# One set of tiles over all 768 tokens, in-products of the groups in two halves of 384 columns, and a written load order for attention

## The chip, the core and the metric

The kernel runs on one core of a Trainium2 chip. The metric is device time in microseconds (us) of one execution; a run is repeated and the median is taken. TensorE does the matmuls (its instruction stream is PE in the profile, its weight loads PEld), VectorE (DVE), ScalarE (ACT) and GpSimd (POOL) do the elementwise work, SyncE (SP) issues the DMAs that bring data from HBM into SBUF. Results of matmuls land in PSUM, from where DVE and ACT take them.

## What is computed

A decayed linear attention over 2 batches, 8 heads, 768 tokens of head size 64, whose output is laid out as 1536 tokens of 512 features; then a gated MLP with 1536 hidden features and an MLP with 2048 hidden features and an ELU between its two matrices:

```
intra = einsum(qb, kb) * Dmask;  intra = einsum(intra, vb)          # per block of 64 tokens
inter = einsum(qb * lam_pow, kv_state)
kv_state = lam_block * kv_state + einsum(kb * rev_pow, vb)
x = attention output, (1536, 512)
x = (sigmoid(x @ w_gate) * (x @ w_val)) @ w_out                     # hidden 1536
h = x @ w_in;  x = where(h > 0, h, exp(min(h, 0)) - 1) @ w_out2     # hidden 2048
```

## The kernel before

All of it is recorded first and ordered afterwards. The code calls operations on a `Work` object, in the order in which they are written; `hazards` works out which operation must follow which, `run` plays the list with a table of costs, `issue` tries some settings and keeps the order with the earliest end. Each engine then gets its instructions in that order, and the real program waits on semaphores. So the order on every engine, SP's DMAs too, is the planner's, not that of the code. Since every operation is issued by one line, the profile's line column says L182 (the line in `call`) almost everywhere, and tiles, not lines, tell the work apart.

The tokens of both batches stand side by side: a tile has 2 batches times 768 tokens, cut in token ranges `s = 0` (256 tokens) and `s = 1` (512 tokens) with a tile each (`NS = (256, 512)`). The attention goes in six chunks `c` of 128 tokens. `scores(c)` makes the masked scores `pr` and the state update (PSUM tiles `st`), then the output of the chunk is summed in PSUM (`x`) from `pr` and the values (`x<-pr,nat`) and from the state `sn` and the decayed queries `ql` (`x<-ql,sn`). Between the two a small ACT operation on the tile `low` stands as a fence. `split_chunk` turns the chunk into a high and a low part (`x11h`, `x11l`, `x143h`, `xPh` and so on), the operands of the MLPs. `kd` are the keys with their decay, made by ACT from `nat`, the loaded keys and values; `tin` holds the loaded transposed keys and queries.

The two MLPs go in groups of 256 hidden features, 6 and 8 of them. A weight is fetched as raw 64-bit words into the one tile `w64` (`w_88`, `w_83` below), made into 32 bits by one ACT and two DVE operations (tile `w`), summed and split into high and low parts `h` and `l` of several tags by POOL, ACT and DVE. An **in-product** (`product`) computes one hidden group for one range of tokens by a scheme of seven products M1 to M7. Each of the seven is six matmuls of 128 by 128 weights (two row blocks `k`, and high times high, high times low, low times high), so 42 matmuls, each as many columns wide as the range has tokens. Their results stand in PSUM banks `A0/B0/C0` or `A1/B1/C1`; the profile's names for them are `warm`, `B` and `st`. DVE and ACT add them up with `wt` and write `sig`, which is split into `gh` and `gl`. An **out-product** (`unit`) multiplies `gh` and `gl` with the output weights `woh`, `wol`, always 512 columns wide (2 batches of 256 tokens), into PSUM tile `xu`; DVE adds it to `acc`.

Groups 1 to 4 of the gated MLP (products G and V) and groups 1 to 6 of the second MLP (product H) use `FULL`, one range of 256 and one of 512 columns; group 0, the last group of the first MLP and the first of the second use three ranges of 256; the last of all uses 512 and 256.

In the attention, chunk 2 is loaded into places of its own (`xPh1` and `sig1`), the others by turns into `gh1` and `gl1` and the two halves of `acc1`. SP waits before a DMA until the old contents of its target have been read.

Of the kernel before, what the change touches and what calls it, by code (L numbers as in the profile page):

```python
# [26 lines left out]
NS = (256, 512)  # L27
# [9 lines left out]
WORDS = 4096  # L37
# [90 lines left out]
class Work:  # L128
    MATMUL = {512: (229, 391), 384: (173, 335), 256: (120, 283)}
# [77 lines left out]
    def hazards(self):  # L207
        write, read, banks, tables = {}, {}, {}, {1: [], 2: []}
        holder, users, freed = {}, {}, {}
        for k, op in enumerate(list(self.ops)):  # L210
# [49 lines left out]
            if op.fence:  # L260
                before.add(self.ops.index(op.fence))
            before -= {-1, k}
            op.preds = sorted(before)

    def run(self, preds, key, backward=False, gate=None, stick=0, thrift=20000):
# [33 lines left out]
        for _ in range(sum(op.eng is not None for op in ops)):  # L299
# [45 lines left out]
            while done:  # L345
                x = done.pop()
                for s in after[x]:
                    f = ops[s].eng
                    ready = free[e] if f == e == "tensor" and x == k else end[x] + self.HANDOFF.get(f, 0)
# [49 lines left out]
def tile_decay_attention_two_mlps(  # L399
# [78 lines left out]
    def new_xops(s):  # L478
        n = NS[s]
        o = {}  # L480
        for t in ("11", "22"):
            for q in "hl":
                o[t, q] = sb.tile([P, 2, n], F32R, f"x{t}{q}{s}")
        for q in "hl":
            o["143", q] = sb.tile([P, 3, 2, n], F32R, f"x143{q}{s}")
            for k, t in enumerate("143"):
                o[t, q] = o["143", q][:, k]
            o["P", q] = sb.tile([P, KC, n], F32R, f"xP{q}{s}")
        return o
# [3 lines left out]
    def x_operand(ops, s, m):  # L493
        o = ops[s]
# [35 lines left out]
    FULL = ((0, 0, 256), (1, 0, 512))  # L530
    PARTS = ((0, 0, 256), (1, 0, 256), (1, 256, 256))

    def product(kind, w, ops, sig, r, which, gsplit=None, two=False):
        s, t0, n = r
        bank, wt = {}, None
        for m in ("M5", "M2") + ORDER[2:] if two else ORDER:
# [9 lines left out]
            bh, bl = (v[:, :, t0:t0 + n] for v in x_operand(ops, s, m))  # L546
# [5 lines left out]
            if wt is None:  # L552
                wt = sb.tile([P, NS[which]], F32, f"wt{which}", bufs=2)[:, :n]
# [5 lines left out]
            else:  # L559
                fh, b = {"M4": (1, 0), "M3": (0, 1), "M7": (0, 0), "M6": (1, 1)}[m]  # L560
                dst = sig[s][:, fh, b, t0:t0 + n]
# [10 lines left out]
                if gsplit is not None and m in ("M7", "M6"):  # L572
                    gsplit(s, fh, t0, n)

    def new_sig():
        return [sb.tile([P, 2, 2, NS[s]], F32, f"sig{s}") for s in range(2)]

# [4 lines left out]
    low = sb.tile([P, 2 * KC * NS[0]], F32, "acc0", name="low")  # L582
    nat = sb.tile([P, 2, 2, 2, H, D], F32, "acc1", name="nat")
# [8 lines left out]
    tin, nat_of = {}, {c: nat[:, int(c in (1, 4))] for c in (0, 1, 3, 4, 5)}  # L592

    def load(c):
        if c == 2:
            tin[c] = sb.tile([P, 2, 2, 2, 2, CH], F32, "xPh1", name="tin2")
            nat_of[c] = sb.tile([P, 2, 2, H, D], F32, "sig1", name="nat2")
        else:
            tin[c] = sb.tile([P, 2, 2, 2, 2, CH], F32, ("gh1", "gl1")[int(c in (1, 4))], name="tin")
        for to, src in ((tin[c].rearrange("p g b q i n -> p (g b q i n)"), att[c, 0]),  # L600
                        (nat_of[c].rearrange("p q b h e -> p (q b h e)"), att[c, 1])):
            for cols in (slice(0, 1024), slice(1024, 2048)) if c < 3 else (slice(0, 2048),):
                nc.sync.dma_start(out=to[:, cols], in_=src[:, cols])

    load(0)
    load(1)
    w64G = load_w(w_gate, 0)
    load(2)
# [36 lines left out]
    xops = [new_xops(0), new_xops(1)]  # L645
    prs, kds, sns = {}, {}, {}
    wG = wV = None
    sig = None
# [8 lines left out]
    def scores(c):  # L657
        prs[c] = []
        if c:
            sns[c] = sb.tile([P, 2, NP, D], F32, f"wt1_{c % 2}", name="sn")  # L660
# [37 lines left out]
    for c in range(NCH):  # L698
        more = c + 1 < NCH
        s, t0 = (0, c * CH) if c < 2 else (1, (c - 2) * CH)  # L700
        scores(c)
        if c in (1, 2, 4):
            load({1: 3, 2: 4, 4: 5}[c])
        if more:
            kd = kds[c] = sb.tile([P, 2, H, D], F32, ("gh0", "gl0")[c % 2], name="kd")
# [40 lines left out]
        split_chunk(xops[s], slice(t0, t0 + CH), xs, xa)  # L746
        if c == 0:
            wG = prep_pair(w_gate, 0, nc.gpsimd, nc.vector, nc.gpsimd, raw=w64G)
        if c == 1:
            wV = prep_pair(w_val, 0, nc.gpsimd, nc.vector, nc.gpsimd)  # L750
            sig = new_sig()
        if c in (1, 3, 5):
            r = PARTS[c // 2]
# [5 lines left out]
    acc = [sb.tile([P, 2, KC, NS[s]], F32, f"acc{s}") for s in range(2)]  # L759

    def new_g(big=None):
        g = []
        for s in range(2):
            if s and big:
                g.append([[sb.tile([P, 2, NS[s]], F32R, f"x{t}{q}{s}", name=f"g{q}{s}") for t in big] for q in "hl"])
            else:
                tl = [sb.tile([P, 2, 2, NS[s]], F32R, f"g{q}{s}") for q in "hl"]
                g.append([[v[:, fh] for fh in range(2)] for v in tl])
        return g

    def splitter(sig, g, eng=None, eng0=None):
        def f(s, fh, t0=0, n=None):
            ts = slice(t0, t0 + (n or NS[s]))
            h, l, x = (v[:, :, ts] for v in (g[s][0][fh], g[s][1][fh], sig[s][:, fh]))
            nc.scalar.copy(h, x)
            ((eng0 if s == 0 else eng) or eng or nc.gpsimd).tensor_tensor(out=l, in0=x, in1=h.bitcast(F32), op=ALU.subtract)
        return f

    def g_cols(t, q, k, t_):
        s = min(t_, 1)  # L780
# [182 lines left out]
```

## Time and profile before

| what | value |
|---|---|
| median of three runs | 587.88 us (585.97 to 589.65) |
| profiled execution, first to last instruction (span) | 583.8 us |
| PE busy | 572.0 us, 98% |
| PEld busy | 491.4 us, 84% |
| DVE, POOL, ACT busy | 388.3, 312.6, 299.5 us (67%, 54%, 51%) |
| granted TensorE clock over the span | 0.999 |
| moved by DMA | 52.03 MB, mean 89 GB/s |

The page gives no time of the profiled execution besides its span; the median of the runs lies 4.1 us above that. A matmul's busy time is longer than the distance to the next one, since matmuls overlap. What one costs in a stream is read from the distance of their starts, or from the chain of waits, which gives a time and a count for each piece.

### The profile page before, as it was taken

The numbers are of one execution on the slowest core, as the hardware profiler recorded it, in microseconds if no ns is written. First come the engines' busy times: TensorE is split into PE (matmuls) and PEld (weight loads), VectorE is DVE, ScalarE is ACT, GpSimd is POOL, SyncE is SP. The second block draws the span as 40 slices with busy tenths as digits, with TensorE's granted clock in tenths as the row PEclk, the third lists the DMA queues.
The fourth block names the chain that finished last, engine by engine and source line by source line (L and its number), as shares of the span: only waits on it lengthen the run. The fifth ranks groups of instructions, "written<-read, shape, count | busy, mean of one in ns | idle before, by whom it ended". The sixth has DMA issues, their size and how long they took to land.

```text
span 583.8 us, 10057 instructions
## 1 busy us (share of the span) xinstructions
PE 572.0 (98%) x4007; PEld 491.4 (84%) x4010; DVE 388.3 (67%) x689; ACT 299.5 (51%) x586; POOL 312.6 (54%) x265
## 2 busy tenths in 40 slices
PE   7799999999999999999999999999999999999997
PEld 5689898888888888888999888888888888888886
DVE  5798653755565565466568985877667767577684
ACT  4784646441532532433347886855555464545360
POOL 1777758466556455565558756545536354514400
PEclk9999999999999999999999999999999999999999
DMA  8954112211212210321210121221121203012014
GB/s 306 413 223 156 64 74 72 82 65 72 87 58 73 76 69 12 132 74 44 101 74 1 72 73 74 73 73 73 72 73 61 85 3 142 1 72 73 0 38 180
DMA packets 9551, 52.03 MB, mean 89 GB/s; under 512 B 1184, under 2 KB 1440, under 8 KB 4384
## 3 DMA queue, kind: packets, MB, share of 16 engines
q1 hardware_dynamic: 9504, 51.39, 24.0%
q8 instruction: 31, 0.51, 0.4%
q14 instruction: 16, 0.13, 0.1%
HBM read 48.24 MB, written 3.15 MB: 88 GB/s over the span
## 4 chain that ended last, share of the span: by engine, by line
PE 92%; DMA 4%; ACT 1%; SPq 1%; DVE 0%; issue 0%; POOL 0%; ACTq 0%
PE xu L182 38%; PE st L182 32%; PE B L182 11%; PE warm L182 9%; DMA nat<-in_att 4%; PE x L182 2%; SPq L182 1%; ACT kd L182 1%; DVE l L182 0%; POOL t L182 0%; DVE o L182 0%; ACT woh L182 0%; ACT h L182 0%; ACT xa L182 0%; ACT x22h L182 0%
## 5 line engine op out<-in xcount | busy, mean ns | idle before, releaser
L182 PE MATMUL xu<-gh,woh 128*128 128x512 f32 (+1 forms) x306 | 119.9, 396 | 0.2
L182 PE MATMUL xu<-gl,woh 128*128 128x512 f32 (+1 forms) x306 | 119.3, 390 | 0.0
L182 PE MATMUL xu<-gh,wol 128*128 128x512 f32 (+1 forms) x306 | 118.9, 389 | 0.0
L182 DVE TENSOR_TENSOR acc<-xu,acc 128x512 f32<-128x512 f32 x120 | 81.9, 687 | 47.0 <-PE xu L182 46.9
L182 POOL TENSOR_TENSOR t<-w 128x256 f32<-128x256 f32 (+1 forms) x80 | 68.3, 880 | 81.0 <-DVE w L182 53.9
L182 POOL TENSOR_TENSOR gl<-sig,gh 128x1024 fp32r<-128x1024 f32 (+1 forms) x38 | 73.2, 1939 | 54.9 <-ACT gh L182 46.8
L182 POOL TENSOR_TENSOR l<-t,h 128x768 fp32r<-128x768 f32 (+1 forms) x38 | 61.2, 1612 | 23.9 <-ACT h L182 11.1
L182 ACT CAST gh<-sig 128x512 fp32r<-128x512 f32 (+1 forms) x58 | 45.2, 787 | 55.2 <-DVE sig L182 55.1
L182 PEld LDWEIGHTS xu<-gh,woh 128*128 128x128 f32 x306 | 57.5, 188 | 14.5 <-DVE acc L182 2.1
L182 PEld LDWEIGHTS xu<-gh,wol 128*128 128x128 f32 x306 | 57.5, 188 | 11.7
L182 PEld LDWEIGHTS xu<-gl,woh 128*128 128x128 f32 x306 | 57.6, 188 | 9.4
L182 ACT ACTIVATE w<-w 128x1024 f32<-128x1024 f32 x34 | 38.7, 1138 | 42.8 <-POOL l L182 28.2
L182 PE MATMUL st<-x143l,h 128*128 128x512 f32 (+1 forms) x150 | 51.9, 346 | 0.0
L182 PE MATMUL st<-x143h,h 128*128 128x512 f32 (+1 forms) x150 | 51.2, 347 | 0.0
L182 PE MATMUL st<-x143h,l 128*128 128x512 f32 (+1 forms) x150 | 51.1, 347 | 0.0
L182 POOL TENSOR_TENSOR wol<-w,woh 128x512 fp32r<-128x512 f32 x26 | 33.1, 1292 | 32.5 <-ACT woh L182 32.0
L182 DVE TENSOR_TENSOR wt<-st,wt 128x512 f32<-128x512 f32 (+1 forms) x57 | 31.9, 560 | 27.6 <-PE st L182 26.1
L182 DVE SCALAR_TENSOR_TENSOR w<-w,w 128x1024 uint32<-128x1024 uint32 x34 | 49.1, 1444 | 0.3
L182 ACT ACTIVATE sig<-st 128x512 f32<-128x512 f32 (+1 forms) x52 | 29.3, 565 | 34.8 <-PE st L182 17.7
L182 DVE TENSOR_SCALAR w<-w 128x1024 uint32<-128x1024 uint32 x34 | 30.7, 903 | 20.7 <-ACT w L182 20.3
L182 ACT ACTIVATE sig<-warm 128x256 f32<-128x256 f32 x36 | 13.8, 384 | 47.7 <-PE warm L182 31.0
L182 ACT ACTIVATE sig<-sig 128x256 f32<-128x256 f32 (+1 forms) x68 | 34.3, 510 | 1.4
(153 smaller groups left out, 1406.9 us busy)
## 6 DMA issues: line engine op xcount, KB each, us to landing
w<-in_w_out SPq DMA_DIRECT2D x14, 1024.0 KB, 4.8
w<-in_w_in SPq DMA_DIRECT2D x8, 1024.0 KB, 4.8
w<-in_w_gate SPq DMA_DIRECT2D x6, 1024.0 KB, 4.7
w<-in_w_val SPq DMA_DIRECT2D x6, 1024.0 KB, 4.9
tin<-in_att SPq DMA_DIRECT2D x6, 512.0 KB, 9.8
nat<-in_att SPq DMA_DIRECT2D x6, 512.0 KB, 11.8
tin<-in_att SPq DMA_DIRECT2D x3, 1024.0 KB, 10.3
nat<-in_att SPq DMA_DIRECT2D x3, 1024.0 KB, 11.3
```

Source lines behind the costliest of these rows:

```text
L182: return [getattr(getattr(self.nc, eng), fn)(*(real(a) for a in args), **{k: real(a) for k, a in kw.items()})]
```

## The change

`NS` goes; each of the operands `x...`, `sig`, `gh`, `gl` and `acc` is one tile over all 768 tokens. `FULL` becomes two ranges of 384 columns each. The three ranges of 256 keep their widths (now called `CHUNKS`), and so does the last group (`ENDS`). Chunk 2's places are gone with the old tiles: its `tin` now goes to `spareh`, where chunk 0's was, and its keys and values into `sig`. The loads are written out in pieces (`t` the transposed keys and queries, `v` the values, `k` the keys), w_val's first group is loaded by name between them, and `hazards` and `run` keep SP's DMAs in the order in which they are written. The planner's cost for a matmul of 384 columns goes from 173 to 171.

```diff
-NS = (256, 512)
+TOK = S
...
-    MATMUL = {512: (229, 391), 384: (173, 335), 256: (120, 283)}
+    MATMUL = {512: (229, 391), 384: (171, 333), 256: (120, 283)}
...
+            if op.eng == "sync":
+                before.add(queued)
+                queued = k
...
-    FULL = ((0, 0, 256), (1, 0, 512))
-    PARTS = ((0, 0, 256), (1, 0, 256), (1, 256, 256))
+    FULL = ((0, 384), (384, 384))
+    CHUNKS = ((0, 256), (256, 256), (512, 256))
+    ENDS = ((256, 512), (0, 256))
...
-    load(0)
-    load(1)
+    load(0, "tv")
     w64G = load_w(w_gate, 0)
-    load(2)
+    load(0, "k")
+    load(1, "tv")
...
         if c in (1, 2, 4):
-            load({1: 3, 2: 4, 4: 5}[c])
+            load({1: 3, 2: 4, 4: 5}[c], "vk")
...
+        if c in (1, 2, 3):
+            load(c + 2, "t")
...
         if c == 0:
             wG = prep_pair(w_gate, 0, nc.gpsimd, nc.vector, nc.gpsimd, raw=w64G)
+            w64V = load_w(w_val, 0)
+            load(1, "k")
+            load(2)
         if c == 1:
-            wV = prep_pair(w_val, 0, nc.gpsimd, nc.vector, nc.gpsimd)
-            sig = new_sig()
+            wV = prep_pair(w_val, 0, nc.gpsimd, nc.vector, nc.gpsimd, raw=w64V)
...
-            for r in FULL:
-                product("G", wG, xops, sig, r, r[0])
-            for r in FULL:
-                product("V", wV, xops, sig, r, r[0], f)
+            for which, r in enumerate(FULL):
+                product("G", wG, xops, sig, r, which)
+            for which, r in enumerate(FULL):
+                product("V", wV, xops, sig, r, which, f)
```

Three places show what the planner makes of it. First PE, in group 1 of the first MLP, where before the gate product's 512 columns end and the value product's 256 begin (`h_465` is a weight part of the gate, `h_648` and `l_669` of the value matrix):

```order
L182 MATMUL st<-xPh_758,h_465 128x512
L182 MATMUL st<-xPl_807,h_465 128x512
L182 MATMUL st<-xPh_758,l_490 128x512
L182 MATMUL warm<-x11h_241,h_648 128x256
L182 MATMUL warm<-x11l_255,h_648 128x256
L182 MATMUL warm<-x11h_241,l_669 128x256
```

and within the gate product of the same group in the changed kernel:

```order
L182 MATMUL B_437<-x143h,h_266 128x384
L182 MATMUL B_437<-x143l,h_266 128x384
L182 MATMUL B_437<-x143h,l_308 128x384
L182 MATMUL st<-x143h,l_461 128x384
L182 MATMUL st<-x143h,h_359 128x384
```

There are as many matmuls as before, 3466 on PE. Of the two widths 588 each (1650 to 1062 of 512, 1272 to 684 of 256) have become 1176 of 384.

Second SP at the program's start, up to the loads of chunk 3, before (`tin_133` and `nat_175` are chunk 2):

```order
L182 DMA lam<-in_lam 128x12
L182 DMA tin<-in_att 128x1024 x2
L182 DMA nat<-in_att 128x1024 x2
L182 DMA tin<-in_att 128x1024
L182 DMA w_88<-in_w_gate 128x2048
L182 DMA tin<-in_att 128x1024
L182 DMA nat<-in_att 128x1024 x2
L182 DMA tin_133<-in_att 128x1024 x2
L182 DMA nat_175<-in_att 128x1024
L182 DMA tin<-in_att 128x2048
L182 DMA nat_175<-in_att 128x1024
L182 DMA w_88<-in_w_val 128x2048
```

and now (`spareh` takes `t` of chunks 0 and 2, `sparel` of chunk 1, `acc` and `sig` take the values and keys):

```order
L182 DMA lam<-in_lam 128x12
L182 DMA spareh<-in_att 128x1024 x2
L182 DMA acc<-in_att 128x1024
L182 DMA w_83<-in_w_gate 128x2048
L182 DMA acc<-in_att 128x1024
L182 DMA sparel<-in_att 128x1024 x2
L182 DMA acc<-in_att 128x1024
L182 DMA w_83<-in_w_val 128x2048
L182 DMA acc<-in_att 128x1024
L182 DMA spareh<-in_att 128x1024 x2
L182 DMA sig<-in_att 128x2x512 x2
```

w_gate is now behind 1.5 MB instead of 2.5 MB, w_val ahead of chunk 1's keys and of all of chunk 2, where it stood behind both and behind a part of chunk 3.

Third ACT while chunk 1 is worked on, before (`w_250` is the weight's 32-bit tile, `low` the fence):

```order
L182 COPY sn<-st 128x2x64
L182 ACTIVATE kd<-nat,low 128x2x64 x2
L182 ACTIVATE low<-low 128x1
L182 ACTIVATE kd<-nat,low 128x2x64 x3
L182 CAST h_371<-w_250 128x256
L182 CAST h_373<-w_250 128x256
L182 COPY xa<-x 128x256 x2
```

and now (`w_199` from `w_83` is w_val, `acc<-acc 128x1` the fence, `sparel` the decayed keys of chunk 1):

```order
L182 COPY wt<-st 128x2x64 x3
L182 ACTIVATE w_199<-w_83 128x1024
L182 ACTIVATE acc<-acc 128x1
L182 CAST h_359<-t_304 128x768
L182 ACTIVATE sparel<-acc 128x2x64 x6
L182 COPY xa<-x 128x256 x2
```

The conversion of w_val, which stood far behind chunk 1's output, now stands ahead of the fence, and six of chunk 1's eight decayed keys stand ahead of the copies out of `x`.

## Rows read from the trace of the kernel before

**Rows 1.** The page's first part: span, and busy time of each engine.

```profile
span 583.8 us, 10057 instructions
PE 572.0 (98%) x4007; PEld 491.4 (84%) x4010; DVE 388.3 (67%) x689; ACT 299.5 (51%) x586; POOL 312.6 (54%) x265
```

**Rows 2.** Busy time by stretch: length, each engine's busy us, granted clock, DMA, GB/s.

```profile
5.00:25.00 20.00, 16.92 (x427) 13.78 (x431) 12.00 (x29) 12.08 (x38) 8.95 (x7) 1.00 1.02 406
25.00:45.00 20.00, 18.25 (x363) 16.07 (x364) 19.45 (x42) 17.32 (x44) 15.54 (x14) 1.00 0.63 248
75.00:285.00 210.00, 210.00 (x1132) 181.53 (x1131) 117.12 (x184) 83.84 (x143) 124.72 (x107) 1.00 0.20 71
345.00:565.00 220.00, 219.98 (x1105) 184.97 (x1104) 154.25 (x238) 124.27 (x223) 102.89 (x83) 1.00 0.17 63
```

**Rows 3.** What PE waited for from 75 us to the end.

```profile
PE st L182 <- ACT x22h L182: 0.9, 1, 0.9
```

**Rows 4.** The chain of waits, 96 to 120 us: start, length, matmuls.

```profile
104.56 7.73 PE st L182 x34
...
113.72 0.72 PE st L182 x6
```

**Rows 5.** PE's instructions in order, 112 to 119 us: start, busy time, operation.

```profile
112.13 0.28 PE L182 MATMUL warm<-x11h,h 128*128 128x256 f32 x1
112.24 0.28 PE L182 MATMUL warm<-x11l,h 128*128 128x256 f32 x1
...
117.14 0.40 PE L182 MATMUL st<-x11h,h 128*128 128x512 f32 x1
117.38 0.39 PE L182 MATMUL st<-x11l,h 128*128 128x512 f32 x1
```

**Rows 6.** DMA issues on SP in the first 25 us: start, length.

```profile
1.16 0.90 SPq L182 DMA_DIRECT2D tin<-in_att  x2
...
15.02 0.33 SPq L182 DMA_DIRECT2D nat<-in_att  x1
19.92 0.33 SPq L182 DMA_DIRECT2D w<-in_w_val  x1
```

**Rows 7.** ACT in order, 9 to 30 us; in brackets its idle time before.

```profile
9.95 2.16 ACT L182 ACTIVATE kd<-nat,low 128x128 f32<-128x128 f32 x7 [4.59 <-DMA nat<-in_att]
...
15.02 1.14 ACT L182 ACTIVATE w<-w 128x1024 f32<-128x1024 f32 x1 [1.55 <-DMA w<-in_w_gate]
...
18.70 0.69 ACT L182 ACTIVATE kd<-nat,low 128x128 f32<-128x128 f32 x2 [0.98 <-DMA nat<-in_att]
...
20.50 0.19 ACT L182 ACTIVATE low<-low 128x1 f32<-128x1 f32 x1
...
22.86 0.38 ACT L182 CAST x11h<-x 128x256 fp32r<-128x256 f32 x1
...
28.94 1.19 ACT L182 ACTIVATE w<-w 128x1024 f32<-128x1024 f32 x1
```

**Rows 8.** DVE in order, 16 to 34 us.

```profile
16.19 0.69 DVE L182 TENSOR_SCALAR w<-w 128x1024 uint32<-128x1024 uint32 x1
...
18.55 1.32 DVE L182 SCALAR_TENSOR_TENSOR w<-w,w 128x1024 uint32<-128x1024 uint32 x1
...
31.61 2.32 DVE L182 SCALAR_TENSOR_TENSOR w<-w,w 128x1024 uint32<-128x1024 uint32 x1
```

**Rows 9.** POOL: the last low parts of w_gate's and w_val's first group.

```profile
28.68 1.84 POOL L182 TENSOR_TENSOR l<-t,h 128x768 fp32r<-128x768 f32 x1 [0.15 <-DVE sn L182]
...
42.67 1.82 POOL L182 TENSOR_TENSOR l<-t,h 128x768 fp32r<-128x768 f32 x1
```

**Rows 10.** PE in order, 5 to 27 us.

```profile
5.40 1.56 PE L182 MATMUL st<-tin 64*64 64x128 f32 x32 [1.90 <-DMA tin<-in_att]
...
16.16 0.90 PE L182 MATMUL st<-tin 64*64 64x128 f32 x32 [1.03 <-DMA tin<-in_att]
...
20.83 1.10 PE L182 MATMUL x<-ql,sn 64*64 64x128 f32 x32 [0.61 <-ACT low L182]
...
26.64 0.38 PE L182 MATMUL warm<-x11l,h 128*128 128x256 f32 x1 [1.27 <-DVE x11l L182]
```

More of the change, by code (lines that the diff above doesn't have):

```diff
@@ L348, in run @@
                     f = ops[s].eng
-                    ready = free[e] if f == e == "tensor" and x == k else end[x] + self.HANDOFF.get(f, 0)
+                    ready = free[e] if f == e and e in ("tensor", "sync") and x == k else end[x] + self.HANDOFF.get(f, 0)
                     at[s] = max(at[s], ready)
@@ L552, in product @@
             if wt is None:
-                wt = sb.tile([P, NS[which]], F32, f"wt{which}", bufs=2)[:, :n]
+                wt = new_wt(which, n)
                 nc.scalar.copy(wt, p)
@@ L572, in product @@
                 if gsplit is not None and m in ("M7", "M6"):
-                    gsplit(s, fh, t0, n)
+                    gsplit(fh, t0, n)
     def new_sig():
-        return [sb.tile([P, 2, 2, NS[s]], F32, f"sig{s}") for s in range(2)]
+        return sb.tile([P, 2, 2, TOK], F32, "sig")
     lo, hi = slice(0, 64), slice(64, 128)
-    low = sb.tile([P, 2 * KC * NS[0]], F32, "acc0", name="low")
-    nat = sb.tile([P, 2, 2, 2, H, D], F32, "acc1", name="nat")
+    acc = sb.tile([P, 2, KC, TOK], F32, "acc")
+    flat = acc.rearrange("p b k n -> p (b k n)")
+    low = flat[:, 0:2048]
+    nat = flat[:, 2048:6144].rearrange("p (c q b h e) -> p c q b h e", c=2, q=2, b=2, h=H)
+    spare = {q: sb.tile([P, 4 * TOK], F32, f"g{q}", name=f"spare{q}") for q in "hl"}
+    xops = new_xops()
+    sig = new_sig()
     da = low[:, 0:768].rearrange("p (f g t n) -> p f g t n", f=2, g=2, t=3)
@@ L590, in tile_decay_attention_two_mlps, with load @@
     nc.sync.dma_start(out=lam_s, in_=lam2)
[L592 to L603, printed above, removed]
-    load(0)
-    load(1)
+    tin, blocks, nat_of = {}, {}, {c: nat[:, int(c in (1, 4))] for c in (0, 1, 3, 4, 5)}
+    def load(c, what="tvk"):
+        if c not in tin:
+            t = spare["hl"[c % 2]][:, 1024:3072].rearrange("p (k x) -> p k x", k=4)
+            if c == 2:
+                n = sig[:, :, :, 256:768]
+                nat_of[c] = n.rearrange("p q b (h e) -> p q b h e", h=H)
+            else:
+                n = nat_of[c].rearrange("p q b h e -> p q b (h e)")
+            tin[c] = t.rearrange("p (g b) (q i n) -> p g b q i n", g=2, q=2, i=2)
+            blocks[c] = t, n
+        t, n = blocks[c]
+        ts, ns = att[c, 0].rearrange("p (k x) -> p k x", k=4), att[c, 1].rearrange("p (q b x) -> p q b x", q=2, b=B)
+        for x in what:
+            if x == "t":
+                for ks in (slice(0, 2), slice(2, 4)) if c < 3 else (slice(0, 4),):
+                    nc.sync.dma_start(out=t[:, ks], in_=ts[:, ks])
+            else:
+                q = int(x == "v")
+                nc.sync.dma_start(out=n[:, q], in_=ns[:, q])
+    load(0, "tv")
     w64G = load_w(w_gate, 0)
-    load(2)
+    load(0, "k")
+    load(1, "tv")
     idle = sb.tile([P, 512], BF16, "xt_2", name="idle")
@@ L659, in scores @@
         if c:
[L660 removed]
+            sns[c] = wts[:, 512 + c % 2 * 512:1024 + c % 2 * 512].rearrange("p (b r e) -> p b r e", b=2, r=NP)
         for g in range(2):
@@ L752, in tile_decay_attention_two_mlps, with new_g @@
         if c in (1, 3, 5):
-            r = PARTS[c // 2]
+            r = CHUNKS[c // 2]
             product("G", wG, xops, sig, r, 0, two=True)
             product("V", wV, xops, sig, r, 0, two=True)
[L759 to L769, printed above, removed]
+    def new_g(big=False):
+        if big:
+            return [[xops[t, q] for t in ("11", "22")] for q in "hl"]
+        tl = [sb.tile([P, 2, 2, TOK], F32R, f"g{q}") for q in "hl"]
+        return [[v[:, fh] for fh in range(2)] for v in tl]
@@ L858, in tile_decay_attention_two_mlps @@
     f = splitter(sig, g)
-    for s in range(2):
+    for r in FULL:
         for fh in range(2):
-            f(s, fh)
+            f(fh, *r)
     wo = prep_out(w_out, 0)
```

68 lines of the change are left out of this document (33 added, 35 removed).

## The prediction

> **What bounds the kernel now.** The page's first part comes first: PE is busy for 572.0 of 583.8 us, and DVE, the next, for 67% [rows 1]. A busy PE isn't yet a bound, so the stretches come next: from 75 to 285 us and from 345 to 565 us PE is busy for 210.00 of 210 and 219.98 of 220 us at a granted clock of 1.00, that is 2.4 GHz, while DVE, ACT and POOL have 30% of it or more to spare [rows 2]. From 75 us to the end PE has one wait on the list, of 0.9 us [rows 3]. So behind 75 us a matmul's cost in a stream is the time, and what the other engines gain there is worth nothing.
>
> That cost is the distance of starts. In the chain of waits a piece of 34 in-product matmuls of 512 columns takes 7.73 us, 227.4 ns each, and a piece of six of 256 columns takes 0.72 us, 120.0 ns each [rows 4]. Single rows agree: 0.11 us apart at 256, 0.24 at 512 [rows 5].
>
> Only the start has slack on PE: from 5 to 25 us it is idle for 3.08 us and from 25 to 45 us for 1.75 us [rows 2]. Before 25 us the DMAs run at 406 GB/s with all queues full [rows 2], and PE waits for what lands; between 25 and 45 us DVE is busy for 19.45 of 20 us.
>
> **The in-products.** 588 matmuls of 256 columns and 588 of 512 become 1176 of 384: 14 products (G and V in groups 1 to 4, H in groups 1 to 6) of 42. A pair costs 120.0 + 227.4 = 347.4 ns now [rows 4]. No matmul of 384 columns is in the trace, so its price is bounded. The straight line through the two widths has a slope of (227.4 - 120.0) / 256 = 0.42 ns a column and gives 120.0 + 128 x 0.42 = 173.7 ns, so 347.4 ns for two: the change is worth nothing, because the columns and the number of matmuls stay the same. The price per column of the wide row, 227.4 / 512 x 384 = 170.6 ns, gives 341.2 ns for two and 588 x 6.2 ns = 3.7 us less. The price per column of the narrow row, 120.0 / 256 x 384 = 180.0 ns, gives 360.0 and 588 x 12.6 ns = 7.4 us more. I take 172.1 ns, half way between the line and the wide row: 384 columns may share the wide row's price more than the narrow one's, but nothing shows that the part of the cost that doesn't grow with the width gets smaller. That is 588 x (347.4 - 344.2) = **1.9 us less**.
>
> The Trainium skill, TensorE: Matmul & The Clock Gate, section Back-to-back issue gap, gives a lone warm matmul of N columns N / 2.4 + 2.5 ns, which is 109.2, 162.5 and 215.7 ns at the three widths: 325 ns for either pair. By it the change would be worth nothing at all; the rows here are 11 to 12 ns above it at both widths, so its constant isn't this kernel's.
>
> What hangs on the in-products isn't on the path. The evictions keep their number and their sum of columns (a DVE or ACT operation of 256 and one of 512 become two of 384), and they lie beside a PE that doesn't wait in rows 3. Out-products stay 512 wide. The out-products of the first 256 tokens need only the first half; those of the next 256 now need both halves, where they needed only the second range. That is the same last product as before, and the four units of the first 256 tokens, six matmuls of 227.4 ns each, are 5.5 us of work that covers its splitting. I put nothing there. The three stages in ranges of 256 and the last group keep their shapes.
>
> **The start.** Here the change moves what waits for what. w_gate stands behind 1 MB less, 2.6 us at 406 GB/s, so it lands at about 12.4 us where ACT got it at 15.02 [rows 7]. Chunk 1's `t` and `v` are behind as many bytes as before; PE got that `t` at 16.16 [rows 10]. w_val must wait on SP until the last reader of w_gate's raw words has ended. Before, that DVE operation ended at 18.55 + 1.32 = 19.87 and SP issued w_val at 19.92 [rows 6, 8]. Now: 12.4 + 1.14 (ACT) + 0.69 (DVE) + 0.4 (one operation of chunk 0 between) + 1.32 = 16.0 us. From issue to the first use a DMA with nothing ahead of it took 4.2 us (1.16, the first issue of `tin`, to 5.40, where PE's wait for it ends) [rows 6, 10]; with 1 MB against its 0.5 MB I put w_val at 21.5 us, where ACT turned to it at 28.94 before [rows 7].
>
> Queued behind w_val on SP are chunk 1's keys and the whole of chunk 2. Chunk 1's keys land at about 22.8 instead of 18.70 [rows 7], and chunk 2's `t` some 3 to 4 us later than before. On ACT the conversion of w_val now stands ahead of the fence: 21.5 + 1.14 = 22.6, fence at 22.7 instead of 20.50 [rows 7], so PE's last pass over chunk 1 begins 2 us later than its 20.83 [rows 10]. ACT then makes `h` and six decayed keys, which need the keys of 22.8, before it copies `x`: some 2.7 us, so `x11h` comes at about 26.3 instead of 22.86 [rows 7]. Behind that `x11l` on DVE, which came late for other reasons before, at about 27.9; it is what PE waited for at 26.64 [rows 10]. **So the stream of the first products starts 1.3 us later.**
>
> Against it stands what w_val brings: its last DVE step ended at 31.61 + 2.32 = 33.9 us [rows 8] and should end at 21.5 + 1.14 + 0.69 + 1.32 = 24.7; its last low part on POOL began at 42.67 [rows 9]. POOL has the first low parts of w_gate, chunk 1's and the queries to do in between, so I see it at 39 to 40 us, 3 to 4 us earlier. PE's idle time from 25 to 45 us was 1.75 us [rows 2], and earlier weights can win back that, and a little of PE's poorly filled time that the busy share hides, but no more. With -1.75 at the one end, and +1.3 and up to 2 us of an empty PE between 23 and 28 us at the other, I take **0**, and -2 to +3 for the range.
>
> **The sum.** 583.8 - 1.9 = 581.9 us of span. The median of the runs lies 4.1 us above the span of the profiled execution, and nothing at either end of the program is changed for that: 586.0 us, 0.3% below 587.88.
>
> **The rivals.** *The half width costs per column as the narrow one does.* That would be so if something that is fixed for two matmuls of 256, such as the way a matmul's columns are fetched, repeats with each 256 begun. For it speaks that the narrow row is the dearer per column (0.469 against 0.444 ns); against it that the fixed part of the line, 13 ns, is the same at both widths. It costs 7.4 us: 595.3 us, slower. It decides from 178.7 ns a matmul on: there 588 x 10 ns make 5.9 us, 1% of the time.
>
> *The half width loses part of the fixed cost.* Single distances of 0.11 us at 256 columns exist [rows 5], where the columns alone are 107 ns at the clock of the rows. With 6.7 ns beside its 160 instead of 13.7, a matmul of 384 would take 166.7 and a pair 333.4: 588 x 14 ns = 8.2 us less, 579.7 us, faster. Against it: such short distances are the exception in the stream.
>
> The 162.5 ns of the Trainium skill's page TensorE: Matmul & The Clock Gate, section Back-to-back issue gap, if the halves alone were to follow them, would be a pair of 325 ns and 13.2 us less, 574.7 us; as no width here follows it, I give that 2 in 100, within this rival's chance.
>
> *The start costs more than the halves win.* If w_val's wait on SP holds chunk 2 back so long that PE runs dry, the upper end of the start's range, +3 us, with the line's price for the halves gives 590.9 us: not faster, within 1%.
>
> *It doesn't do what it says* can't be in the widths: the rows of the order show them. It can be in the time, as the straight line says: 587.9.
>
> **How the numbers follow.** Forecast, with the line's case and the costlier start, 0.75 together (the last two rivals 0.3 of it); the shorter halves 0.15; the dearer ones 0.10. 586.0 is the likeliest case. From it: the wide row's price and the best start give 583.8 - 3.7 - 2 + 4.1 = 582.2, the line and the worst start 590.9; the range reaches a little into both other cases, 580.5 to 592. About 1%, 5.9 us, is what a measurement of this kernel tells from no change. Faster by that (under 582.0) 0.16 (the shorter halves and the forecast's own lower edge), slower (over 593.8) 0.09 (most of the dearer halves), within it 0.75.
>
> **What would show it.** In the profile after: starts of in-product matmuls of 384 columns 171 to 174 ns apart, in pieces of the chain as the 227.4 ns were read; PE busy for all of the stretch from 75 us on, with no new wait over 1 us; w_gate converted on ACT near 12.4 us and w_val near 21.5; the fence of chunk 1 near 22.7; the first stream of products near 27.9. The forecast is wrong if the distance is under 168 or over 178 ns, if PE waits somewhere behind 75 us for halves that share a tile, or if PE is idle for over 5 us between 20 and 45 us.

## The result and the profile after

The changed kernel takes 590.78 us (median, 590.21 to 592.42), and its ratio to the kernel before is 1.0065 [1.0047, 1.0083]: 0.65% slower, where 0.3% faster was forecast. (The quotient of the two medians alone is 1.0049, which the interval holds.) The time lies inside the range of 580.5 to 592, the sign is wrong, and with the ends of the interval the change is a small loss and not a tie. The profiled execution took 590.8 us over a span of 589.0, where the one before had 583.8 [rows 1].

Each execution whose span is listed took 1.8 us more than its span, as this one did. So the 4.1 us between the median and the span of the kernel before, which the forecast added, aren't that distance: the profiled execution of the kernel before was some 2.3 us faster than its median. The 5.2 us between the two spans are therefore more than the difference in time, which is 2.9 us by the medians and 3.8 by the ratio.

The page's first part, of the changed kernel:

```profile
span 589.0 us, 10097 instructions
PE 575.6 (98%) x4008; PEld 515.3 (87%) x4010; DVE 385.5 (65%) x689; ACT 301.3 (51%) x586; POOL 305.2 (52%) x265
```

PE does the same matmuls, 3.6 us more of busy time in a span that is 5.2 us longer. The price of a half is the first thing to look up. The chain of waits of the changed kernel, 95 to 240 us (start, length, matmuls), has pure pieces of 384 columns, the longest of them:

```profile
108.00 7.28 PE st L182 x42
```

7.28 / 42 = 173.3 ns: the straight line's 173.7 ns, where 172.1 was taken. Over all 1077 pairs of neighbours of this width in the trace the distance has a median of 173 ns and a mean of 174.4 ns. The same count in the kernel before, from 90 us on, has means of 120.8 ns at 256 columns and 228.5 at 512: 349.3 ns for such a pair, against 348.8 for two halves. So two halves cost what 256 and 512 did, and the loss isn't in the width.

For the rest the span is split in two kinds of time. PE's in- and out-products are 128 x 128 matmuls of known width and distance: 1272 of 256 columns and 1632 of 512 before, 684, 1044 and 1176 of 384 after. (Left out are 18 more of 512 columns in each kernel, on a tile of zeros named `idle`, which run before the first product.) At 120.0, 227.4 and 173.7 ns each kernel has 523.8 us of them, the same sum. All else is called **lost time** here: attention, waits, gaps. Before 90 us the kernel before had begun 261 of 256 columns and 35 of 512, 39.3 us of products, so 50.7 us were lost by then; the changed kernel had begun 252 and 22, 35.2 us, and lost 54.8. The rest of the span less the rest of the products is 9.3 us before and 10.5 after. So **4.1 us of the 5.2 between the spans are lost by 90 us**, 1.1 behind it.

Busy time by stretch of the changed kernel (length, each engine's busy us, granted clock, DMA share, GB/s), which answers to [rows 2]:

```profile
5.00:25.00 20.00, 14.56 (x360) 10.98 (x360) 13.92 (x30) 13.15 (x37) 8.43 (x7) 1.00 0.97 364
25.00:45.00 20.00, 18.30 (x326) 16.00 (x327) 12.57 (x35) 15.23 (x44) 16.68 (x14) 1.00 0.61 235
75.00:285.00 210.00, 209.37 (x1118) 193.27 (x1118) 124.03 (x190) 89.62 (x149) 130.85 (x114) 1.00 0.22 76
345.00:565.00 220.00, 219.72 (x1101) 195.52 (x1102) 150.57 (x236) 122.36 (x218) 93.09 (x78) 1.00 0.17 58
```

From 5 to 25 us PE is idle for 5.44 us instead of 3.08. From 25 to 45 us it is idle for 1.70 us, where it was 1.75, so what earlier weights were to win back there stayed lost. The two long stretches stay full. What the prediction worked out by hand for the start came nearly to pass. ACT in order, of the changed kernel, for [rows 7]:

```profile
11.06 1.13 ACT L182 ACTIVATE w<-w 128x1024 f32<-128x1024 f32 x1 [5.80 <-DMA w<-in_w_gate]
...
20.09 1.17 ACT L182 ACTIVATE w<-w 128x1024 f32<-128x1024 f32 x1 [0.29 <-POOL t L182]
21.16 0.19 ACT L182 ACTIVATE acc<-acc 128x1 f32<-128x1 f32 x1
...
24.52 0.38 ACT L182 CAST x11h<-x 128x256 fp32r<-128x256 f32 x1
```

With the forecast in brackets: w_gate at 11.06 us (12.4), w_val at 20.09 (21.5), the fence at 21.16 (22.7), `x11h` at 24.52 (26.3). The stream of the first products began at 27.65 us (27.9), behind two single matmuls at 26.60 and 26.82, and V's last low part on POOL came at 39.88 (39 to 40):

```profile
27.65 0.39 PE L182 MATMUL warm<-x11l,h 128*128 128x256 f32 x1
```

One part of it cost PE time. Chunk 2's `t` and keys, behind w_val on SP, came late, as was forecast. PE waited for the `t` at 23.88 us and again for 0.38 us at 25.16; ACT waited for the keys until 27.84, and a copy that ACT had to make behind them held PE up for 1.5 us. The wait of 1.27 us for `x11l` in the kernel before [rows 10] is gone in exchange. Of the changed kernel, PE and ACT in order, and PE's waits from 25 to 90 us (us in total, times, longest):

```profile
23.88 0.90 PE L182 MATMUL st<-spareh 64*64 64x128 f32 x32 [0.98 <-DMA spareh<-in_att]
27.84 0.70 ACT L182 ACTIVATE spareh<-sig,acc 128x128 f32<-128x128 f32 x2 [1.75 <-DMA sig<-in_att]
PE B L182 <- ACT wt L182: 1.5, 1, 1.5
```

By the marks, the lost time before and after is 24.9 and 25.0 us at 25 us, 37.9 and 36.6 at 45, 44.9 and 45.6 at 60, 50.3 and 53.1 at 75. The lead at 45 us is only apparent: the changed kernel had then begun 608 of the 1088 matmuls of attention and the kernel before 720, so it had put off work that was still to come. PE's idle time is free of that. With the matmuls on `idle` counted as idle, it is 10.7 us before and 12.5 after by 25 us, then 1.7 and 1.8 us from 25 to 60, and none and 1.1 us from 60 to 90. That makes 3.0 of the 4.1 us, more of it ahead of 25 us than behind 60; the rest lies in time that counts as busy. The stretch from 65 to 90 us, of the kernel before and of the changed one:

```profile
65.00:90.00 25.00, 25.00 (x243) 22.42 (x243) 14.27 (x32) 14.28 (x28) 17.45 (x16) 1.00 0.12 44
65.00:90.00 25.00, 23.87 (x233) 20.61 (x234) 14.70 (x36) 14.00 (x31) 20.22 (x17) 1.00 0.27 86
```

The last chunks of attention end late: the last attention matmul runs at 72.5 us, before at 67.9. POOL in order there, of the changed kernel:

```profile
71.68 3.62 POOL L182 TENSOR_TENSOR gl<-sig,gh 128x768 fp32r<-128x768 f32 x2
```

Group 0's `g` is split by FULL, so its low part waits for 384 tokens and is 768 wide; before, 512 wide, it was begun at 63.7 us. PE took up the first out-products with low parts behind it. POOL in order, of the kernel before:

```profile
63.72 2.54 POOL L182 TENSOR_TENSOR gl<-sig,gh 128x512 fp32r<-128x512 f32 x2
```

What PE waited for from 75 us to the end, the longest, for [rows 3]:

```profile
PE st L182 <- POOL wol L182: 0.4, 1, 0.4
```

Nothing there is over 1 us, as forecast.

### The profile page after: what moved, and what is told of

Same layout as the page of the kernel before. It is cut to its first block, busy times and chain, and to the rows that moved or that the text cites. A ratio compares the mean times of both kernels' runs of the same rounds, so it can differ in the third digit from the quotient of the medians.

```text
span 589.0 us, 10097 instructions
## 1 busy us (share of the span) xinstructions
PE 575.6 (98%) x4008; PEld 515.3 (87%) x4010; DVE 385.5 (65%) x689; ACT 301.3 (51%) x586; POOL 305.2 (52%) x265
## 4 chain that ended last, share of the span: by engine, by line
PE 91%; DMA 4%; DVE 2%; POOL 2%; ACT 1%; SPq 1%; issue 0%; DVEq 0%; POOLq 0%
PE xu L182 37%; PE st L182 28%; PE B L182 13%; PE warm L182 12%; DMA sparel<-in_att 2%; DMA sig<-in_att 2%; PE x L182 2%; SPq L182 1%; ACT spareh L182 0%; POOL l L182 0%; DVE pr L182 0%; POOL gl L182 0%; POOL x143l L182 0%; POOL t L182 0%; DVE xu L182 0%
## 5 line engine op out<-in xcount | busy, mean ns | idle before, releaser
L182 PE MATMUL xu<-gl,woh 128*128 128x512 f32 x296 | 116.1, 392 | 0.0
L182 PE MATMUL xu<-gh,wol 128*128 128x512 f32 x296 | 116.0, 392 | 0.0
L182 PE MATMUL xu<-gh,woh 128*128 128x512 f32 x296 | 114.2, 395 | 0.3 <-DVE xt L182 0.3
L182 POOL TENSOR_TENSOR gl<-sig,gh 128x768 fp32r<-128x768 f32 (+1 forms) x38 | 67.8, 1788 | 78.3 <-ACT gh L182 41.7
L182 PEld LDWEIGHTS xu<-gh,wol 128*128 128x128 f32 x296 | 55.6, 188 | 10.6
L182 PEld LDWEIGHTS xu<-gl,woh 128*128 128x128 f32 x296 | 55.6, 188 | 8.5
L182 ACT CAST gh<-sig 128x768 fp32r<-128x768 f32 (+1 forms) x56 | 44.1, 792 | 35.6 <-DVE sig L182 35.3
L182 PE MATMUL st<-x143l,h 128*128 128x384 f32 (+2 forms) x150 | 48.9, 327 | 0.3 <-POOL x143l L182 0.3
L182 PE MATMUL st<-x143h,h 128*128 128x384 f32 (+2 forms) x150 | 48.6, 327 | 0.0
L182 PE MATMUL st<-x143h,l 128*128 128x384 f32 (+2 forms) x150 | 48.1, 326 | 0.0
L182 DVE TENSOR_TENSOR wt<-st,wt 128x384 f32<-128x384 f32 (+2 forms) x57 | 30.1, 527 | 26.1 <-PE st L182 24.7
L182 ACT CAST h<-t 128x512 fp32r<-128x512 f32 (+1 forms) x40 | 29.0, 726 | 23.5 <-POOL t L182 23.2
```

The costliest lines, as they stand in the source:

```text
L182: return [getattr(getattr(self.nc, eng), fn)(*(real(a) for a in args), **{k: real(a) for k, a in kw.items()})]
```

## The experiments

Ratios are to the kernel before, with 95% intervals, from five rounds each. Lost time is as defined above, by 90 us and behind it, from the profiled execution of each (the changed kernel: 54.8 and 10.5 us; the kernel before: 50.7 and 9.3). The first theory was that the start costs it, by the order of the loads or by the halves; the rival that the halves or the shared tiles cost throughout.

**e1, the old widths in the changed kernel.**

```diff
-    FULL = ((0, 384), (384, 384))
+    FULL = ((0, 256), (256, 512))
```

> The changed kernel with the two ranges of 256 and 512 columns again in place of the halves; tiles, places and load order stay. Theory 'start' (the loss lies before 80 us, in what the loads make late; 173 ns for 384 columns is the straight line): no change against the changed kernel, ratio to before 1.005 to 1.008. Rival 'widths' (the halves cost more than their columns): back to before, ratio 0.999 to 1.002.

1.0044 [1.0029, 1.0059], between the two cases, lost 52.7 and 11.0 us. It gives back 2.1 us of the start and nothing behind it, so no cost of the halves in the streams shows. Since the splitting of group 0's `g` goes by `FULL`, the edit alters that too.

**e2, the loads free.** SP's loads keep their places and pieces, but aren't chained to one another.

```diff
-            if op.eng == "sync":
-                before.add(queued)
-                queued = k
...
```

> The changed kernel without the written order of SP's DMAs: the planner sorts them again, so the output weights of group 0 come ahead of chunk 5's loads (in its order they stand 6 DMAs earlier) and the first value weights behind chunk 2. Theory 'queue' (the written order holds the output weights and all that follow in their one tile behind chunk 5's loads): most of the loss is gone, ratio 0.999 to 1.003. Rival 'place' (chunk 2 in chunk 0's place makes chunk 4 late): it stays, 1.005 to 1.008.

1.0024 [1.0011, 1.0037], lost 52.9 and 9.6 us: a good part of the loss went.

**e3, w_out earlier.** In the changed kernel w_out is issued at 54.24 us on SP, before at 34.01. It was put ahead of the later loads:

```diff
...
             wV = prep_pair(w_val, 0, nc.gpsimd, nc.vector, nc.gpsimd, raw=w64V)
+            w64O = load_w(w_out, 0)
...
-    wo = prep_out(w_out, 0)
+    wo = prep_out(w_out, 0, raw=w64O)
```

> The changed kernel with the output weights of group 0 loaded ahead of chunk 4's and 5's last loads, still in a written order; one DMA is moved. Theory 'queue': they land some 20 us sooner than at 62.6, and the time falls by 2 to 3 us, ratio 1.001 to 1.004. If it is not they but the gate weights of group 1, still behind chunk 5, that PE lacks, the ratio stays at 1.005 to 1.007. Rival 'place': also stays.

SP in order, of this kernel, shows that the edit did what it says:

```profile
23.94 0.33 SPq L182 DMA_DIRECT2D w<-in_w_out  x1
```

Yet 1.0087 [1.0069, 1.0104], over all its cases, and lost 56.3 us by 90. So a late w_out isn't shown to be the cause.

**e4, chunk 2's place alone,** in the kernel before.

```diff
-            tin[c] = sb.tile([P, 2, 2, 2, 2, CH], F32, "xPh1", name="tin2")
...
+            tin[c] = sb.tile([P, 2, 2, 2, 2, CH], F32, ("gh1", "gl1")[c % 2], name="tin")
...
+        if c in (1, 2, 3):
+            load(c + 2, "t")
```

> The kernel before with one part of the change: chunk 2's transposed keys and queries go into chunk 0's place, 3's into 1's and so on; order of SP free, widths and tiles as before. Rival 'place': chunk 4's land near 42 us where they landed at 31.35, and 2 to 4 us are lost, ratio 1.003 to 1.007. Theory 'queue': PE has other work meanwhile, ratio 0.998 to 1.002.

0.9984 [0.9974, 0.9995], lost 50.7 and 9.6 us. The place shows no cost.

**e5 and e6, the two halves of the change apart.** e5 is the kernel before with the new loads: order, pieces, places of `t` and chain. e6 is the changed kernel with the old first loads and free order:

```diff
-    load(0, "tv")
+    load(0)
+    load(1)
     w64G = load_w(w_gate, 0)
-    load(0, "k")
-    load(1, "tv")
...
-            w64V = load_w(w_val, 0)
-            load(1, "k")
```

> The kernel before with the loads of the change: the same written order, pieces and places of chunks, DMAs kept in order on SP; the tiles stay cut in 256 and 512 tokens, the widths too. Theory 'queue' (the written order makes the loss at the start): the loss comes with it, ratio 1.003 to 1.007. Rival 'tiles' (what the whole tiles tie together makes it): none, 0.998 to 1.002. Rival 'scatter' (any edit shifts the planner's choice of order by 1 to 2 us): anywhere from 0.998 to 1.007, and no part can be named from one kernel.

> The changed kernel with the loads of before: free order on SP, the first loads as they were, w_val fetched where its weights are made; whole tiles, halves of 384 and chunk 2 in chunk 0's place stay. Theory 'queue': no loss, ratio 0.998 to 1.002. Rival 'tiles': the loss stays, 1.003 to 1.007; as the kernel with free loads alone measured 1.0024, a ratio near that says that the first loads don't matter and the tiles cost 1 to 2 us.

e5: 1.0028 [1.0016, 1.0040], lost 52.5 and 9.4 us. e6: 1.0057 [1.0043, 1.0071], lost 54.3 and 9.2. Alone, the tiles with the halves seemed to cost nearly all of it, and the loads 0.3%.

**e7 and e8, one number of the planner.** The diff also set the planner's price of 384 columns to 171 ns. e7 puts 173 there, e8 puts 121 for 120 at 256 columns:

```diff
-    MATMUL = {512: (229, 391), 384: (171, 333), 256: (120, 283)}
+    MATMUL = {512: (229, 391), 384: (173, 335), 256: (120, 283)}
```

> The changed kernel with the planner's old cost of 173 for a matmul of 384 columns instead of 171: same loads, same first 170 instructions on PE, another order behind. Theory 'queue' and rival 'tiles': as the changed kernel, ratio 1.005 to 1.008. Rival 'scatter': it moves by 1 us or more, to 1.002 to 1.005 or over 1.008.

> The changed kernel with the planner's cost of a matmul of 256 columns at 121 instead of 120: same operations and loads, only the planner's order differs, from the 90th instruction of PE on. Theory 'queue' and rival 'tiles': ratio 1.005 to 1.008 as the changed kernel. Rival 'scatter': 1 us or more away from it.

e7: **1.0135** [1.0119, 1.0151], lost 55.2 and 12.6 us; e8: 1.0057 [1.0044, 1.0070], 54.8 and 9.9. Tiles, widths and loads are the same; only the order that the planner draws from its costs is another. Two nanoseconds moved the time by 0.7%, as much as the whole change. From here on a single run of an edit could no longer be read as that edit's cost.

**e9 to e11, the split of group 0's g.** The theory by now: the first out-products start late because `g` is split by halves.

```diff
-    for r in FULL:
+    for r in ((0, 256), (256, 512)):
         for fh in range(2):
             f(fh, *r)
```

e9 is that edit in the changed kernel, e10 has the loads free as well, e11 is e6 with the old widths (tiles without halves).

> The changed kernel with one line of group 0 altered: its g is split into parts of 256 and 512 tokens again, so that the first out-products wait for 256 tokens and not for 384. Theory 'split' (the start's loss is the late and wide split of g): its low part is made some 4 to 9 us earlier than the 73.5 us of the changed kernel, the time that PE lost by 90 us falls from 54.8 to about 52.5 us, ratio 1.002 to 1.004. Rival 'scatter' (any change of the order moves the time by up to 0.7%, and no one wait is the cause): the lost time stays above 54 us, or falls without regard to when g's part is made, ratio 1.005 or more. Rival 'loads' (the load order alone is the whole loss): unchanged, 1.0065.

> The kernel of the run before this one, and SP's loads again free in their order (no chain between one load and the next). If split and load order add up: lost time by 90 us 50.7 to 51.5 us, ratio 0.997 to 1.001. If the load order's part was already in the 52.9 us that free loads alone gave: about as that run, 1.002. If scatter rules: anywhere from 0.998 to 1.008.

> One set of tiles over all 768 tokens, with the ranges of 256 and 512, the old first loads and SP's free order: the tiles without the halves. If the shared tiles cost nothing and the halves in the start did: lost time by 90 us about 50.7 to 51.5 us, ratio 0.998 to 1.002. If the shared tiles themselves cost (a writer of one range waits for readers of the other): as the tiles with halves, 54.4 us and 1.005 to 1.006.

e9: 1.0031 [1.0014, 1.0048], lost 52.6 and 9.9 us. POOL in order, of e9:

```profile
60.49 1.29 POOL L182 TENSOR_TENSOR gl<-sig,gh 128x512 fp32r<-128x512 f32 x1
```

That is 11 us earlier than in the changed kernel (4 to 9 were expected), and the 2.2 us that the theory asked for came back. e10: 1.0022 [1.0011, 1.0033], 51.9 us; split and free loads don't add up (52.6 and 52.9 alone). e11: 1.0031 [1.0019, 1.0042], 53.0 and 10.2 us: not the 50.7 to 51.5 of tiles that cost nothing.

**e12, the kernel before with 121 ns,** as e8.

> The kernel before with one number of the planner altered by 1 ns: 121 for 120 ns a matmul of 256 columns. It computes the same with the same tiles and loads; only the order that the planner draws from its costs differs. If orders scatter: a ratio off 1.000 by 0.002 to 0.008, on either side, with the lost time by 90 us or behind it moved by 1 us or more. If the order of before is no lucky draw but what these costs give whatever the nanosecond: 0.999 to 1.001.

1.0032 [1.0020, 1.0044], lost 53.8 and 9.3 us. The same kernel in another order loses 3 us in the start. What PE waited for by 90 us, of e12, the longest:

```profile
PE st L182 <- issue: 4.6, 2, 3.5
```

**e13 to e16, the split once more, from other orders.** e9's edit in e8 (e13), in e6 (e14) and in e7 (e15), and the reverse edit, two halves of 384, in e11 (e16).

> The changed kernel with the planner's 121 for 120 ns (lost time by 90 us 55.0 us, ratio 1.0057) and group 0's g split by 256 and 512 tokens. Theory 'split': the lost time by 90 us falls by about 2.2 us, as it did in the first trial of this edit (54.8 to 52.6), to 52.3 to 53.3 us; ratio 1.002 to 1.004. Rival 'scatter' (the first trial was a lucky order): the lost time falls by less than 1 us, or rises.

> The tiles and halves without the new load order (lost time by 90 us 54.4 us, ratio 1.0057), and group 0's g split by 256 and 512. Theory 'split': 51.7 to 52.7 us, ratio 1.001 to 1.003. Rival 'scatter': less than 1 us of fall, or a rise. Beside the kernel with ranges of 256 and 512 throughout and the same loads (1.0031) it also tells what the halves do behind the start: if they cost or bring nothing, equal lost time from 90 us to the end within 1 us.

> The changed kernel with the planner's 173 for 171 ns (lost time by 90 us 55.3 us and 9.0 us more behind it, ratio 1.0135) and group 0's g split by 256 and 512. Theory 'split': lost time by 90 us 52.6 to 53.6 us. If the 3 us that this kernel lost late in the program were an accident of its order, they may be gone in this order (5.6 to 6.9 us from 90 us to the end, ratio 1.002 to 1.005); if the cost of 173 itself brings them, 9 us stay and the ratio is about 1.010. Rival 'scatter': no fall by 90 us.

> The reverse: the kernel with tiles over all 768 tokens and ranges of 256 and 512 throughout (lost time by 90 us 53.0 us, ratio 1.0031), but group 0's g split by two halves of 384. Theory 'split': the lost time rises by about 2 us to 54.5 to 55.5 us, ratio 1.006 to 1.008, with g's first low part on POOL 768 wide and behind 70 us. Rival 'scatter': less than 1 us of rise, or a fall, ratio 1.001 to 1.004.

| edit | ratio without | ratio with the split at 256 | lost by 90 us, without and with |
|---|---|---|---|
| changed kernel, e9 | 1.0065 | 1.0031 | 54.8, 52.6 |
| free loads (e2), e10 | 1.0024 | 1.0022 | 52.9, 51.9 |
| 121 ns (e8), e13 | 1.0057 | 1.0093 [1.0074, 1.0111] | 54.8, 55.6 |
| tiles (e6), e14 | 1.0057 | 1.0082 [1.0065, 1.0099] | 54.3, 54.2 |
| 173 ns (e7), e15 | 1.0135 | 1.0111 [1.0092, 1.0130] | 55.2, 57.4 |
| e16 against e11 | 1.0068 [1.0049, 1.0086] | 1.0031 | 54.3, 53.0 |

The changes of lost time are -2.2, -1.0, +0.8, -0.1, +2.2 and -1.3 us: mixed signs and a mean of -0.3. e16 by itself came out as the theory had it (1.0068 in its 1.006 to 1.008, the low part 768 wide and at 71.08 us, the lost time just under its range); e13, e14 and e15 went against it. **As the account of the loss the theory of the split falls.** In e13 the low part of `g` is narrow and still begins only at 69.47 us, in e15 at 72.83, of POOL in order:

```profile
72.83 2.53 POOL L182 TENSOR_TENSOR gl<-sig,gh 128x512 fp32r<-128x512 f32 x2
```

When it is made is for the planner's order to say, not for the width of the split. So e13 and e15 tell against the edit; what a low part made early is worth by itself they don't test. e15 also says that e7's 12.6 us behind 90 us weren't the price of 173 itself: they are 9.8 there.

**e17 and e18, two more neighbours of the kernel before:** 230 for 229 ns at 512 columns, and 119 for 120 at 256.

```diff
-    MATMUL = {512: (229, 391), 384: (173, 335), 256: (120, 283)}
+    MATMUL = {512: (229, 391), 384: (173, 335), 256: (119, 282)}
```

> The kernel before with the planner's 230 for 229 ns a matmul of 512 columns, and nothing else. If the kernel before is a favourable order among its own neighbours, as its neighbour at 121 ns showed (1.0032): slower again, 1.002 to 1.008. If that neighbour was an accident and orders scatter evenly about the kernel before: 0.997 to 1.002.

> The kernel before with the planner's 119 for 120 ns a matmul of 256 columns, and nothing else. The same two cases: 1.002 to 1.008 if the kernel before is a favourable order, 0.997 to 1.002 if orders scatter evenly about it. With the neighbour at 121 ns and the one of this call there are then three neighbours of before beside its own; if their mean is about that of the kernels with shared tiles and halves (1.007), the change has no cost of its own at all, if it is about 1.003, the change costs some 0.4% beside the scatter.

e17: 1.0014 [1.0004, 1.0023], lost 52.5 and 9.2 us. e18: **0.9961** [0.9949, 0.9973], 583.96 us, the fastest of all and faster than either of its two cases had it. Its span is 582.9 us. Of its stretches, the one with a lower granted clock:

```profile
25.00:45.00 20.00, 18.47 (x365) 16.51 (x367) 16.00 (x38) 15.12 (x38) 14.00 (x13) 0.91 0.51 196
```

It loses 52.2 us by 90, more than the kernel before, and 6.9 behind it: its gain is late. Some 1.6 of these 2.4 us lie between the matmuls of the out-products, whose starts from 90 us on are 229.2 ns apart in the mean of 847 pairs, and 231.1 ns (844 pairs) in the kernel before. The three neighbours have a mean of 1.0002, so the kernel before is no lucky draw among them.

**The draws side by side:**

| kernels | n | ratio, mean (lowest to highest) | lost by 90 us | lost behind |
|---|---|---|---|---|
| before, e12, e17, e18: the kernel before in four orders | 4 | 1.0002 (0.9961 to 1.0032) | 52.3 | 8.7 |
| e4, e5: old tiles, with the new place or loads | 2 | 1.0006 (0.9984, 1.0028) | 51.6 | 9.5 |
| e1, e11, e16: shared tiles, widths 256 and 512 | 3 | 1.0048 (1.0031 to 1.0068) | 53.3 | 10.4 |
| changed, e2, e3, e6 to e10, e13 to e15: shared tiles and halves | 11 | 1.0069 (1.0022 to 1.0135) | 54.5 | 10.4 |

The last row against the first: 0.0067, with standard deviations of 0.0036 over 11 and 0.0030 over 4, so 0.0067 ± 0.0045 (t at some 6 degrees of freedom). The eleven aren't plain repeats, since edits are in them, but only two of the fourteen kernels with shared tiles come in under 1.003 (e2 and e10, both with free loads) and only one of the six without comes in over it.

Over the 20 profiles the lost time by 90 us goes with the time of the last attention matmul (66.2 to 76.2 us; correlation 0.91), more closely than with that of group 0's first low part (59.6 to 73.2 us; 0.77). That names no cause, but it says what to look at: what makes attention end late.

## Why the prediction was wrong

**The sign failed in "I take 0, and -2 to +3 for the range", the start's term.** The trace shows +4.1 us by 90 us. The 0 set a gain against a loss: earlier weights were to win back PE's 1.75 us of idle time from 25 to 45 us. V's last low part did come 2.8 us earlier (39.88 us instead of 42.67), but 1.70 us of the idle time stayed, and by 25 us PE had been idle for 1.8 us more than before. The hand-run ended at 28 us, with an outlook on one operation at 40, and every date in it held within 2 us, most of them early. It then took the rest of the start, up to the last attention matmul, as unmoved. That matmul came 4.6 us later, and PE was idle for another 1.1 us between 60 and 90 us. A list of what moves at the front of a queue doesn't price a stage in which a planner reorders all five engines.

**A term was missing: the order as a whole.** In the experiments the order alone moved the time from -0.4% to +0.3% about the kernel before (four orders) and from 1.0057 to 1.0135 in the changed kernel (171 and 173 ns, 120 and 121). No bound of the prediction allowed for that. These are spreads of 4.2 and 4.6 us, where the range reaches 5.75 us either way from its middle and the largest term of the sum is 1.9 us.

**The halves, -1.9 us, should have been 0.** The pieces of the chain give 173.3 ns, so the line held and "half way between the line and the wide row" had no ground. At the line's price the forecast would have been 583.8 + 4.1 = 587.9 us, no change. Both rivals on the width fall: 173.3 ns lies far from 166.7 and from 180. The Trainium skill's N / 2.4 + 2.5 ns for a lone matmul (TensorE: Matmul & The Clock Gate, section Back-to-back issue gap) makes an estimate of 162.5 ns for 384 columns; the chain shows 10.8 ns more, as it showed 11 to 12 at the other widths, so for this stream the measurement decides against its constant, and not against its slope.

**"I put nothing there"**, on the out-products that now wait for both halves and on the splitting: not shown to be wrong. Group 0's split is late in the changed kernel, and putting it back helped by 2.2 us there and by 1.0 with free loads, but the same edit from three other orders gave +0.8, -0.1 and +2.2.

**The rival "the start costs more than the halves win", 590.9 us, came closest** to 590.78, by the place and the amount; its mechanism is shown in part. It had w_val's wait on SP hold chunk 2 back, and PE's 0.98 and 0.38 us for chunk 2's `t` and 1.5 us behind ACT are such waits. But only those ahead of 25 us add to PE's idle time, since the 1.5 us stand where the kernel before had a wait of 1.27 us [rows 10]; and e5, which has this order of loads in the kernel before, is no slower than a neighbouring order of it (1.0028, beside 1.0032). So the new loads aren't shown to cost anything on the whole, and neither is chunk 2's place (e4). That 590.9 meets 590.78 so closely is luck: orders of the changed kernel run from 1.0057 to 1.0135.

**The other steps.** No wait over 1 us came behind 75 us, PE stayed full there, and the number of DVE and ACT operations is unchanged, 689 and 586. The forecast's own mark of failure, "if PE is idle for over 5 us between 20 and 45 us", never came: it was idle there for 3.4 us, before for 2.6. The mark asked for one long gap, and the loss is a sum of small ones.

**What stays open** is which part of the change makes the loss. Shared tiles with halves lose 3.9 us more than four orders of the kernel before, 2.2 us by 90 us and 1.7 behind it; the 1.7 rest in part on e18 (6.9 us; the other three orders have 9.2 to 9.3). Shared tiles with the old widths have the same 1.7 behind and 1.0 by 90 us; with three draws that can't be told from scatter, nor can what the halves add. Nor are these three quite the old widths: the change also puts the sums `wt` into one tile, where a range of 512 has one place, and before it had two by turns.

Two rivals aren't settled. One is the chain between SP's loads. e2 and e10, the changed kernel's tiles, halves and loads without it, are the two lowest of the eleven (1.0024 and 1.0022), and the seven with it have 1.0031 to 1.0135, a mean of 1.0083; e6 and e14, without it and with the old first loads, have 1.0057 and 1.0082. The other is the tiles. By the code of `hazards`, two ranges don't bind each other by standing in one tile, since it follows a tile by its columns; only where a slot changes its shape or type does it wait for all that the slot held. That is so for group 0's `gh` and `gl`, which follow `spareh` and `sparel`: no low part can begin until chunk 5's `t`, in `sparel`, has been read. In the kernel before, the first 256 tokens of `gh` and `gl` followed decayed keys alone. That this costs anything is argued from the code and not shown. Telling the two apart would take several orders of each kernel.

## What to carry to other kernels

Where a planner sets the order, change one of its costs by a nanosecond and time that before pricing an edit: here the same kernel spread over 0.7%, and the best of those draws (0.9961 [0.9949, 0.9973]) beat every deliberate edit. An edit's cost is then the difference between several orders with it and several without, and a theory of one wait is to be tried from more than one order; the split of `g` fitted its first trial to the tenth of a microsecond and came out otherwise from the next three orders (e13 to e15). Between two measured widths take the straight line for a third until a row says otherwise: here it held within 0.4 ns (173.3 against 173.7).

## What the runs showed of the hardware

The granted clock fell in the start of 12 of the 20 profiles, that of the fastest kernel among them: 0.91 from 25 to 45 us in e18, where the kernel before kept 1.00 [rows 2]. By the stretches of 1 us of e18, of PE alone (length, busy us, granted clock, DMA share, GB/s):

```profile
29.00:30.00 1.00, 0.00 (x0) 1.00 0.97 406
30.00:31.00 1.00, 0.80 (x18) 1.00 1.01 426
31.00:32.00 1.00, 1.00 (x18) 0.57 1.03 426
32.00:33.00 1.00, 1.00 (x17) 0.50 1.01 426
```

PE stands idle from 28.7 to 30.2 us, and within a microsecond of taking up work again it runs at 0.50, that is 1.2 GHz, until it is back at 2.4 between 34 and 35 us (0.72 over that microsecond). At 45 us e18 has lost 38.5 us where the kernel before had lost 37.9, and it still ends earlier. The loss of the changed kernel isn't made by such falls: its two executions with a mean granted clock of 1.000 took 590.78 and 590.89 us, the three with 0.994 took 590.21, 590.22 and 592.42. They may add to the spread, though: beside e1 to e4, the two executions of the kernel before at 0.993 took 588.96 and 589.13 us, where the median of all 23 was 586.47. And the lost time of a single profile carries them: in e15 the clock fell twice, in the changed kernel never.

The distance of streamed matmuls has a constant part of 13 to 14 ns at 256, 384 and 512 columns alike (120.0, 173.3 and 227.4 ns, less 106.7, 160.0 and 213.3 ns of columns at 2.4 GHz).
